# Decoding the MLP weights in half-width pieces inside the rounds, and moving reload transfers to GpSimd's queue

## The chip, the cores and the metric

One core of one Trainium2 chip runs one program. The metric is the device time of one execution in microseconds (us). The engines are TensorE (PE, matmul; PEld is its weight load), VectorE (DVE), ScalarE (ACT), GpSimd (POOL) and SyncE (SP, which here only starts transfers). Each engine works through its own list of instructions in order. A transfer (DMA) is started from the list of one engine, and an engine that waits to start one holds up everything behind it on its list.

## The reference

Attention with a sigmoid, a gated layer, then a residual MLP. The change touches the last part alone:

```python
x = moe(attention(q, k, v))              # (4, 448, 768)
xn = (x - mean) / sqrt(var + 1e-6) * g_ln
out = x + maximum(xn @ w_ch1, 0) @ w_ch2   # w_ch1 768x3072, w_ch2 3072x768
```

The weights arrive as float64. The kernel sees them as pairs of 32-bit words and makes float32 of them on the chip ("decode").

## The kernel before

The matmuls are done in three passes (`mm3`, lines 268 to 271): each float32 operand is split in a high and a low part (`split`: a copy on ACT, line 298, and a subtraction, line 299 on DVE or line 733 on GpSimd).

**The rounds.** `mlp` runs 24 rounds: two halves `h` of the tokens, and in each half twelve groups `g` of hidden columns (`GF * g` and the next). A round `k` makes the group's hidden activations by seven products `P_` (a Strassen-Winograd form: L11, L12, S2, S1, S3, L22, S4, each 9 matmuls of 448 columns) and, between and after them, the seven chunks of the second matrix multiply for the round before (`ch2_chunks`: 12 matmuls of 384 columns per chunk, then one addition of the 128x768 result onto `y`, line 790 on DVE). In a common round the first chunk (c1) stands between the products S3 and L22 and the other six (c2 to c7) follow the last product. Two buffers (`ps2`) hold chunk results, so the matmuls of c4 can start only when the addition of c2 is done, those of c5 after c3's addition, and so on. A round is followed in the trace from one copy of line 863 to the next.

**The decoded weights.** Each weight is a 128x768 block. The first half of the tokens needs every group's four blocks (two of `w_ch1`, two of `w_ch2`) decoded; decoded blocks are written to a scratch tensor `wscr` and read back by `Weight.load` (line 723), for both halves. Groups 0 to 4 are decoded during the attention phase. Groups 5 to 11 (28 blocks) are decoded in rounds 1 to 10 by the jobs of `pre_jobs`: `load` (line 279, 768 KB from `in_w`), `decode` (`w_decode`: line 287 on ACT, then lines 288, 289 and 292 on DVE) and `store` (line 348, 384 KB). `pre.pop(n)` takes the next n jobs and writes their instructions into the lists of the engines at that place. Before the change there is one raw buffer (`pre_start`), so a step is decode, store, load of the next block, and the rounds hold nine pops, that is three blocks a round. The order of the instructions is written out by hand (`manual_schedule`).

**What is queued on SP.** The store waits for the decode and the load waits for the raw buffer; behind them on SP's list stand the `Weight.load`s of the round: `w2c.load`, `w2d.load` and the next round's two (`nxt.load`).

**The handover between the halves.** In round 11 (`h` = 0, the last group) `ops_load` (line 1125) replaces each operand of the products by that of the other half, 1344 KB each, seven in all, as soon as its product is done. Round 12 starts with six chunks of round 11, whose sums go to the output (line 796), then `y_load` (line 1155) reads the other half's `y`, seven times 384 KB. All of these are started by SP.

Of the kernel before, what the change touches and what calls it, by code (L numbers as in the profile page):

```python
# [11 lines left out]
F32 = mybir.dt.float32  # L12
# [22 lines left out]
GF = 2  # L35
# [126 lines left out]
class Ring:  # L162
# [4 lines left out]
    def next(self):  # L167
        self.i += 1
        return self.blocks[(self.i - 1) % len(self.blocks)]
# [54 lines left out]
def sigmoid_attention_gmlp_mlp(ctx: ExitStack, tc, q, k, v, w_in, w_sp, w_out, g_ln, w1, w2, out):  # L224
# [50 lines left out]
    dec_r = Ring(F, WC, 2)  # L275

    def w_load(src, ring=raw_r):
        raw = ring.next().bits(WC, 2)
        nc.sync.dma_start(raw.rearrange("p n t -> p (n t)"), src.bitcast(U32))
        return raw  # L280

    def w_decode(raw, blk=None):
        blk = blk or dec_r.next()
        f, bits = blk.ap(WC), blk.bits(WC)
        low, high = raw[:, :, 0], raw[:, :, 1]

        nc.scalar.mul(f, high.bitcast(F32), 2.0**-112)  # L287
        nc.vector.tensor_scalar(bits, bits, 3, None, op0=ALU.logical_shift_left)  # L288
        nc.vector.scalar_tensor_tensor(  # L289
            bits, low, 29, bits, op0=ALU.logical_shift_right, op1=ALU.bitwise_or  # L290
        )
        nc.vector.scalar_tensor_tensor(  # L292
            bits, high, 0x80000000, bits, op0=ALU.bitwise_and, op1=ALU.bitwise_or
        )
        return f
# [38 lines left out]
    def pre_jobs(todo, raws, decs):  # L334

        raw, f = {}, {}
        n = len(todo)

        def load(w, i):
            raw[w, i] = w_load((w1, w2)[w][i], raws)  # L340

        def decode(w, i):
            blk = decs.next()
            f[w, i] = blk.ap(WC)
            w_decode(raw.pop((w, i)), blk)

        def store(w, i):
            nc.sync.dma_start(wscr[w, i], f.pop((w, i)))

        if len(raws.blocks) > 1:  # L350
            steps = (load, 0), (store, 3), (decode, 2)
        else:
            steps = (decode, 1), (store, 1), (load, 0)
        for m in range(n + 3):
            for job, i in steps:
                if 0 <= m - i < n:
                    yield functools.partial(job, *todo[m - i])
                else:
                    yield idle

    def weights_of(groups):
        return [(w, GF * g + i) for g in groups for w in range(2) for i in range(GF)]

    jobs = Jobs()

# [400 lines left out]
    def mlp(first, proj, after):  # L766
# [58 lines left out]
        for k, (h, g) in enumerate(todo):  # L825
# [48 lines left out]
            if k == 0:  # L874
                left.put("S4")
                proj.turn()
                nxt.sums(nc.vector)
            P_(pa, "S2", "T2", False)
            nc.scalar.copy(tb, pa[:, :S])
            pre.pop(1)  # L880
            pd = ps1()
            P_(pd, "S1", "T1", True)
            pre.pop(2)
            if nxt and k:
                nxt.sums()
            P_(pa, "S3", "T3", False)
            nc.scalar.copy(tc_, pa[:, :S])
            nc.vector.tensor_add(tc_, pd[:, :S], tc_)
# [5 lines left out]
            if k:  # L894
                w2c.load()
                if nxt:
                    nxt.put("L11")
            P_(pa, "L22", "T4", False)
            put(1, 0, pa[:, :S])
            if nxt:  # L900
                nxt.put("L12" if k else "S2")
# [1 line left out]
            P_(pd, "S4", "R22", False)  # L903
            nc.vector.tensor_add(tb, pd[:, :S], tb)  # L904
            put(0, 1, tb)
            pre.pop(2)
            if k == 0:
                nxt.put("S1", "S3")
                w2c.load()
                w2d.load()  # L910
                y_start()
                nxt.put("L22", "S4")
                w2c.split()
                w2d.split()
                pre_start()
            else:
                if h and g == 0:
                    for c in range(HCH):
                        y_load(1, c)
                if nxt:  # L920
                    nxt.put("S2")
                next(chunks, None)
                if nxt:
                    nxt.put("S1", "S3")
                next(chunks, None)
                if nxt:
                    nxt.put("L22", "S4")
                w2d.load()
                next(chunks, None)
                pre.pop(1)  # L930
                next(chunks, None)
                w2c.split()
                next(chunks, None)
                pre.pop(2)
                for _ in chunks:
                    pass
                late = w2d
            chunks, pend = ch2_chunks(h, g, hb, second), True
            left = nxt
# [30 lines left out]
    pv_load(1)  # L970
    jobs.pop(1)
    pre = Jobs()
    pre.add(pre_jobs(weights_of(range(NPRE)), p_raw, p_dec))
    for i in range(2 * n_pairs):
        p, t = divmod(i, 2)
        now[0] = i
# [144 lines left out]
    def ops_load(name):  # L1121

        n = OPS.index(name)
        place, at = PLACE_OPS[n]
        nc.sync.dma_start(R.tiles[place][:, at : at + OPW].bitcast(F32), oscr[n])

    ops_at(*range(6))
    proj = Project(wo, gb, ys_r, xn_r, stage_r, t_b, t4_b)
# [22 lines left out]
    ys = [None] * HCH  # L1151
    pre = Jobs()

    def y_load(h, c):
        nc.sync.dma_start(ys[c].ap(DM), yscr[h * HCH + c])

    def y_start():

# [6 lines left out]

    def pre_start():
        raws, decs = Ring(F, 0, 0), Ring(F, 0, 0)
        raws.blocks, decs.blocks = [F.at("mlp", 3072, 2 * WC)], [F.at("mlp", 4608, WC)]
        decs.blocks.append(next(t for t in dec.q if t.key == "mlp"))
        dec.q.remove(decs.blocks[1])  # L1170
        pre.add(pre_jobs(weights_of(range(NPRE, NGRP)), raws, decs))

    mlp(left, proj, after)

# [46 lines left out]
```

## Time and profile before

| | us |
|---|---|
| median of 3 runs | 1169.75 (1168.42 to 1169.81) |
| the profiled execution | 1166.97 |
| its span (first to last instruction) | 1165.2 |
| TensorE busy | 1082.0 (93%) |
| VectorE busy | 674.5 (58%) |
| ScalarE busy | 457.1 (39%) |
| GpSimd busy | 315.7 (27%) |

Busy times are unions over the span. A busy TensorE is not necessarily at full speed: the granted clock (1.00 is 2.4 GHz, 0.50 is 1.2 GHz) has to be read beside it. Positions are given in us from the start of the span. The table of stages gives for each stretch the busy time of each engine and the clock; the rows of the order of time show which instruction ended an engine's idle time, in brackets.

### The profile page before, as it was taken

To read this page: it belongs to the slowest core of one execution; us is meant where nothing else is said; L and a number is where in the kernel's file an instruction comes from. 1 tells how busy PE (TensorE), PEld (TensorE's weight loads), DVE (VectorE), ACT (ScalarE), POOL (GpSimd) and SP (SyncE) were. 2 spreads that over 40 slices of the span, in tenths; PEclk is the share of its full clock that TensorE was granted. 3 is DMA by queue.
4 is the path that set the end of the run, shared out by engine and by line. 5 is a ranking of instruction groups with operands and counts; after the bars stand their busy time and mean duration, and the time that the engine had idled before them with its cause. 6 is when DMAs were issued, how large, how long until landed. Compare 5 with 4: busy or idle time off the path is not lost.

```text
span 1165.2 us, 14921 instructions
## 1 busy us (share of the span) xinstructions
PE 1082.0 (93%) x5644; PEld 950.1 (82%) x5644; DVE 674.5 (58%) x988; ACT 457.1 (39%) x792; POOL 315.7 (27%) x278
## 2 busy tenths in 40 slices
PE   8999999999999689888898788898899999999997
PEld 4566666679899578788898788898799999999997
DVE  4734536446767757676666676654355555555543
ACT  6755556554566643233222233230322332333310
POOL 1322212212047433122233022322133222222210
PEclk9999999999999889989988889998999999999999
DMA  8756779735224673534443534366521111111103
GB/s 236 232 176 215 246 235 332 233 141 188 75 83 175 240 270 122 176 120 165 141 158 122 176 119 166 133 245 232 196 68 55 55 55 55 55 58 65 55 28 95
DMA packets 65112, 174.52 MB, mean 150 GB/s; under 512 B 11664, under 2 KB 23312, under 8 KB 64016
## 3 DMA queue, kind: packets, MB, share of 16 engines
q1 hardware_dynamic: 62320, 164.11, 41.9%
q0 software_dynamic: 1600, 7.34, 1.9%
q10 hardware_dynamic: 1120, 2.11, 0.5%
q8 instruction: 44, 0.72, 0.3%
q14 instruction: 28, 0.23, 0.1%
HBM read 126.67 MB, written 46.87 MB: 149 GB/s over the span
## 4 chain that ended last, share of the span: by engine, by line
PE 63%; DVE 11%; DMA 10%; issue 5%; ACT 5%; POOL 3%; SPq 2%; POOLq 0%; ACTq 0%; DVEq 0%
PE ps L269 18%; PE ps L270 17%; PE ps L271 17%; PE ps L463 5%; PE ps L447 5%; DMA f_mlp<-in_w 4%; DMA f_base<-wscr 2%; DVE f_mlp L289 2%; DVE f_mlp L292 2%; DVE f_mlp L288 2%; ACT f_mlp L287 1%; ACT f_mlp L678 1%; DMA sscr<-vraws 1%; DVE f_base L790 1%; DMA wscr<-f_att 1%
## 5 line engine op out<-in xcount | busy, mean ns | idle before, releaser
L269 PE MATMUL ps<-r_mlp,r_base 128*128 128x384 f32 (+1 forms) x946 | 340.6, 360 | 55.3 <-DVE f_base L790 41.2
L270 PE MATMUL ps<-r_mlp,r_base 128*128 128x384 f32 (+1 forms) x946 | 336.7, 356 | 2.6 <-POOL r_mlp L733 2.6
L271 PE MATMUL ps<-r_mlp,r_base 128*128 128x384 f32 (+1 forms) x946 | 336.2, 355 | 0.0
L269 PEld LDWEIGHTS ps<-r_mlp,r_base 128*128 128x128 f32 x946 | 186.9, 198 | 66.1 <-DVE f_base L790 44.4
L733 POOL TENSOR_TENSOR r_mlp<-f_base,r_mlp 128x768 fp32r<-128x768 f32 x48 | 88.4, 1843 | 529.2 <-ACT r_mlp L732 529.2
L270 PEld LDWEIGHTS ps<-r_mlp,r_base 128*128 128x128 f32 x946 | 186.8, 197 | 6.9 <-POOL r_mlp L733 3.3
L271 PEld LDWEIGHTS ps<-r_mlp,r_base 128*128 128x128 f32 x946 | 186.4, 197 | 3.0
L790 DVE TENSOR_TENSOR f_mlp<-ps,f_mlp 128x768 f32<-128x768 f32 (+1 forms) x97 | 91.6, 947 | 78.0 <-PE ps L271 77.7
L269 PE MATMUL ps<-r_base 128*128 128x448 f32 (+1 forms) x348 | 132.4, 380 | 1.3 <-ACT r_base L298 1.3
L271 PE MATMUL ps<-r_base 128*128 128x448 f32 (+1 forms) x348 | 130.1, 374 | 0.4 <-DVE r_base L299 0.4
L270 PE MATMUL ps<-r_base 128*128 128x448 f32 (+1 forms) x348 | 129.9, 373 | 0.0
L451 ACT ACTIVATE f_att<-ps,bias_s 128x896 f32<-128x896 f32 x96 | 91.5, 1006 | 25.9 <-PE ps L447 25.5
L863 ACT COPY f_base<-ps 128x448 f32<-128x448 f32 x24 | 12.8, 533 | 221.5 <-PE ps L271 221.5
L790 DVE TENSOR_TENSOR f_base<-ps,f_base 128x768 f32<-128x768 f32 x72 | 68.6, 953 | 30.7 <-PE ps L271 29.9
L850 ACT ACTIVATE r_base<-f_base 128x448 fp32r<-128x448 f32 x72 | 41.6, 578 | 113.2 <-DVE f_base L904 54.4
L447 PEld LDWEIGHTS ps<-r_att 64*128 64x128 f32 x576 | 49.8, 184 | 36.9 <-issue 19.7
L447 PE MATMUL ps<-r_att 64*128 64x448 f32 x576 | 73.7, 383 | 6.4 <-ACT f_att L451 4.4
L269 PEld LDWEIGHTS ps<-r_base 128*128 128x128 f32 x348 | 65.5, 188 | 15.5 <-issue 6.5
L463 PE MATMUL ps<-f_att 128*64 128x448 f32 x384 | 77.5, 545 | 0.0
L434 POOL TENSOR_TENSOR r_att<-f_att,r_att 128x512 fp32r<-128x512 f32 x22 | 29.9, 1359 | 174.9 <-DVE r_att L430 147.0
L271 PEld LDWEIGHTS ps<-r_base 128*128 128x128 f32 x348 | 65.6, 189 | 8.6 <-DVE r_base L299 0.8
L851 DVE SCALAR_TENSOR_TENSOR r_base<-f_base,r_base 128x448 fp32r<-128x448 f32 x72 | 50.5, 701 | 37.2 <-ACT r_base L850 37.2
(127 smaller groups left out, 1551.1 us busy)
## 6 DMA issues: line engine op xcount, KB each, us to landing
f_base<-wscr SPq DMA_DIRECT2D x95, 384.0 KB, 5.0
f_mlp<-in_w SPq DMA_DIRECT2D x28, 768.0 KB, 4.8
f_att<-in_w SPq DMA_DIRECT2D x20, 768.0 KB, 5.6
wscr<-f_mlp SPq DMA_DIRECT2D x28, 384.0 KB, 2.6
wscr<-f_att SPq DMA_DIRECT2D x20, 384.0 KB, 6.0
f_att<-in_v SPq DMA_DIRECT2D x24, 256.0 KB, 5.4
f_base<-in_w_in SPq DMA_DIRECT2D x8, 768.0 KB, 4.7
f_att<-in_k SPq DMA_DIRECT2D x45, 128.0 KB, 5.2
```

The source lines that it names most:

```text
L269: nc.tensor.matmul(ps, lh, rh, start=first, stop=False, **more)
L270: nc.tensor.matmul(ps, lh, rl, start=False, stop=False, **more)
L271: nc.tensor.matmul(ps, ll, rh, start=False, stop=last, **more)
L288: nc.vector.tensor_scalar(bits, bits, 3, None, op0=ALU.logical_shift_left)
L434: eng.tensor_sub(kl, kr, kh)
L447: nc.tensor.matmul(ps[:, j, :S], a[w][rows, kc], a[x][rows], start=(i == 0), stop=(i == 2))
L451: nc.scalar.activation(af, ps[:, :, :S], AF.Sigmoid, bias=bias_s, scale=1.0 / math.sqrt(D))
L463: nc.tensor.matmul(a["ps"][rows, :S], a["v"][:, 4 * j + c], af[:, j], start=(c == 0), stop=(c == 3))
L733: nc.gpsimd.tensor_sub(self.lo, self.blk.ap(WC), self.hi)
L790: nc.vector.tensor_add(y[:, hs], ps, y[:, hs])
L850: nc.scalar.activation(hi, src, AF.Relu)
L851: nc.vector.scalar_tensor_tensor(lo, src, 0.0, hi, op0=ALU.max, op1=ALU.subtract)
```

## The change

Jobs work on a piece, a slice of 384 columns of a block, instead of the whole block. `pre_start` cuts the same memory into two raw buffers and four decoded ones. The steps become decode of piece m-2, store of piece m-2, load of piece m. The rounds hold 18 pops instead of nine (six pieces, which are three blocks), set so that a decode is popped alone and a store and a load together. `ops_load` and the second half's `y_load` are started by GpSimd instead of SP. The decoding in the attention phase keeps whole blocks and its order (`weights_of(..., WC)`, three raw buffers).

```diff
 def w_load(src, ring=raw_r):
-        raw = ring.next().bits(WC, 2)
+        raw = ring.next().bits(src.shape[-1], 2)
 def w_decode(raw, blk=None):
         blk = blk or dec_r.next()
-        f, bits = blk.ap(WC), blk.bits(WC)
+        n = raw.shape[1]
+        f, bits = blk.ap(n), blk.bits(n)
 def pre_jobs(todo, raws, decs):
-        def load(w, i):
-            raw[w, i] = w_load((w1, w2)[w][i], raws)
+        def load(w, i, cols):
+            raw[w, i, cols] = w_load((w1, w2)[w][i][:, cols], raws)
...
-        if len(raws.blocks) > 1:
+        if len(raws.blocks) > 2:
             steps = (load, 0), (store, 3), (decode, 2)
         else:
-            steps = (decode, 1), (store, 1), (load, 0)
+            steps = (decode, 2), (store, 2), (load, 0)
...
-    def weights_of(groups):
-        return [(w, GF * g + i) for g in groups for w in range(2) for i in range(GF)]
+    def weights_of(groups, n):
+        cuts = [slice(o, o + n) for o in range(0, WC, n)]
+        return [(w, GF * g + i, cut) for g in groups for w in range(2) for i in range(GF) for cut in cuts]
 def mlp(first, proj, after):                # one round
+            pre.pop(1)
             P_(pa, "S2", "T2", False)
             nc.scalar.copy(tb, pa[:, :S])
-            pre.pop(1)
             P_(pd, "S1", "T1", True)
             pre.pop(2)
...
+            pre.pop(1)
             P_(pa, "S3", "T3", False)
...
             P_(pa, "L22", "T4", False)
+            pre.pop(2)
             put(1, 0, pa[:, :S])
...
             pre.pop(1)
             P_(pd, "S4", "R22", False)
             nc.vector.tensor_add(tb, pd[:, :S], tb)
             put(0, 1, tb)
-            pre.pop(2)
...
                     for c in range(HCH):
-                        y_load(1, c)
+                        y_load(1, c, nc.gpsimd)
+                pre.pop(2)
                 nxt.put("S2")
                 next(chunks, None)          # c2
+                pre.pop(1)
                 nxt.put("S1", "S3")
                 next(chunks, None)          # c3
+                pre.pop(2)
                 nxt.put("L22", "S4")
                 w2d.load()
                 next(chunks, None)          # c4
                 pre.pop(1)
                 next(chunks, None)          # c5
                 w2c.split()
+                pre.pop(2)
                 next(chunks, None)          # c6
-                pre.pop(2)
+                pre.pop(1)
                 for _ in chunks: pass       # c7
+                pre.pop(2)
 def ops_load(name):
-        nc.sync.dma_start(R.tiles[place][:, at : at + OPW].bitcast(F32), oscr[n])
+        nc.gpsimd.dma_start(R.tiles[place][:, at : at + OPW].bitcast(F32), oscr[n])
 def pre_start():
-        raws.blocks, decs.blocks = [F.at("mlp", 3072, 2 * WC)], [F.at("mlp", 4608, WC)]
-        decs.blocks.append(next(t for t in dec.q if t.key == "mlp"))
-        dec.q.remove(decs.blocks[1])
-        pre.add(pre_jobs(weights_of(range(NPRE, NGRP)), raws, decs))
+        raws.blocks = F.at("mlp", 3072, 2 * WC).cut(WC, WC)
+        decs.blocks = F.at("mlp", 4608, WC).cut(HALF, HALF)
+        last = next(t for t in dec.q if t.key == "mlp")
+        dec.q.remove(last)
+        decs.blocks += last.cut(HALF, HALF)
+        pre.add(pre_jobs(weights_of(range(NPRE, NGRP), HALF), raws, decs))
```

## Rows read from the trace of the kernel before

**Rows 1.** Stages: us, busy of PE, PEld, DVE, ACT, POOL, granted clock, DMA share, GB/s.

```profile
424.60:771.00 346.40, 301.71 (x1463) 286.28 (x1464) 232.06 (x294) 105.61 (x188) 90.85 (x61) 0.91 0.42 150
771.00:868.20 97.20, 88.05 (x443) 83.53 (x442) 44.47 (x63) 24.65 (x49) 23.54 (x18) 0.95 0.57 205
868.20:1117.50 249.30, 249.30 (x1325) 239.93 (x1324) 134.86 (x189) 73.92 (x145) 72.33 (x54) 1.00 0.17 58
```

**Rows 2.** Order of time in round 6: start, length, instruction, idle before and its releaser.

```profile
606.59 0.37 SPq L279 DMA_DIRECT2D f_mlp<-in_w  x1
611.10 0.91 ACT L287 ACTIVATE f_mlp<-f_mlp 128x768 f32<-128x768 f32 x1 [2.24 <-DMA f_mlp<-in_w]
612.03 0.56 DVE L288 TENSOR_SCALAR f_mlp<-f_mlp 128x768 uint32<-128x768 uint32 x1 [2.45 <-ACT f_mlp L287]
614.50 0.62 DVE L904 TENSOR_TENSOR f_base<-ps,f_base 128x448 f32<-128x448 f32 x1
616.77 0.95 DVE L790 TENSOR_TENSOR f_base<-ps,f_base 128x768 f32<-128x768 f32 x1
617.77 0.69 PE L269 MATMUL ps<-r_mlp,r_base 128*128 128x384 f32 x1 [3.82 <-DVE f_base L790]
```

**Rows 3.** Waits over the span: who for whom, us in total, times, longest.

```profile
ACT f_mlp L287 <- DMA f_mlp<-in_w: 43.9, 18, 4.8
```

**Rows 4.** TensorE's gaps in rounds 2 and 1, and the stretches behind them.

```profile
488.52 0.44 PE L269 MATMUL ps<-r_mlp,r_base 128*128 128x384 f32 x1 [1.17 <-DVE f_mlp L790]
488.50:492.80 4.30, 4.28 (x23) 4.13 (x24) 1.79 (x2) 0.00 (x0) 0.00 (x0) 1.00 1.00 333
444.41 0.45 PE L269 MATMUL ps<-r_mlp,r_base 128*128 128x384 f32 x1 [2.00 <-DVE f_base L790]
445.40:448.80 3.40, 3.40 (x12) 3.40 (x12) 2.60 (x5) 1.64 (x2) 0.55 (x1) 0.50 0.37 148
```

**Rows 5.** Groups by shape, whole span: count, busy us, mean ns, idle before.

```profile
L790 DVE TENSOR_TENSOR f_mlp<-ps,f_mlp 128x384 f32<-128x384 f32 x2 | 1.1, 558 | 0.6 <-PE ps L271 0.5
```

**Rows 6.** VectorE in round 15, which decodes nothing, in order of time.

```profile
908.20 0.55 DVE L299 TENSOR_TENSOR r_base<-f_base,r_base 128x384 fp32r<-128x384 f32 x1
908.88 0.62 DVE L904 TENSOR_TENSOR f_base<-ps,f_base 128x448 f32<-128x448 f32 x1
...
911.16 0.95 DVE L790 TENSOR_TENSOR f_base<-ps,f_base 128x768 f32<-128x768 f32 x1
912.03 1.02 DVE L299 TENSOR_TENSOR r_base<-f_base,r_base 128x384 fp32r<-128x384 f32 x2
913.11 0.96 DVE L790 TENSOR_TENSOR f_base<-ps,f_base 128x768 f32<-128x768 f32 x1
913.99 1.26 DVE L299 TENSOR_TENSOR r_base<-f_base,r_base 128x384 fp32r<-128x384 f32 x1
...
917.35 0.96 DVE L790 TENSOR_TENSOR f_mlp<-ps,f_mlp 128x768 f32<-128x768 f32 x1 [0.77 <-PE ps L271]
919.47 0.96 DVE L790 TENSOR_TENSOR f_mlp<-ps,f_mlp 128x768 f32<-128x768 f32 x1 [1.16 <-PE ps L271]
```

**Rows 7.** Order of time, rounds 12 and 13: TensorE's gaps, SP's first `y` loads.

```profile
800.34 0.69 PE L269 MATMUL ps<-r_mlp,r_base 128*128 128x384 f32 x1 [3.04 <-ACT r_mlp L732]
802.23 0.69 PE L270 MATMUL ps<-r_mlp,r_base 128*128 128x384 f32 x1 [1.20 <-POOL r_mlp L733]
830.83 1.41 SPq L1155 DMA_DIRECT2D f_base<-yscr  x3
844.13 0.47 PE L269 MATMUL ps<-r_mlp,r_base 128*128 128x448 f32 x1 [3.99 <-ACT f_base L879]
```

**Rows 8.** Chain of waits: start, length, the transfers of rounds 11 and 13.

```profile
784.51 14.85 DMA f_base<-wscr
...
834.78 7.54 DMA f_base<-wscr
```

**Rows 9.** Line 279 in rounds 2 to 10: us from issue to landing.

```profile
DMA to landing us min/median/max: 4.4/4.8/7.0
```

**Rows 10.** Line 1030, GpSimd's own transfers of 768 KB: issue ns, min/median/max.

```profile
L1030 POOL DMA_DIRECT2D f_mlp<-vscr x4: 762/786/925, 249.6 to 284.8; - x4
```

More of the change, by code (lines that the diff above doesn't have):

```diff
@@ L337, in pre_jobs, with decode, store @@
         n = len(todo)
-        def load(w, i):
-            raw[w, i] = w_load((w1, w2)[w][i], raws)
-        def decode(w, i):
+        def load(w, i, cols):
+            raw[w, i, cols] = w_load((w1, w2)[w][i][:, cols], raws)
+        def decode(w, i, cols):
             blk = decs.next()
[L344 to L348, printed above, removed]
-        if len(raws.blocks) > 1:
+            w_decode(raw.pop((w, i, cols)), blk)
+            f[w, i, cols] = blk.ap(cols.stop - cols.start)
+        def store(w, i, cols):
+            nc.sync.dma_start(wscr[w, i][:, cols], f.pop((w, i, cols)))
+        if len(raws.blocks) > 2:
             steps = (load, 0), (store, 3), (decode, 2)
         else:
-            steps = (decode, 1), (store, 1), (load, 0)
+            steps = (decode, 2), (store, 2), (load, 0)
         for m in range(n + 3):
@@ L972, in sigmoid_attention_gmlp_mlp @@
     pre = Jobs()
-    pre.add(pre_jobs(weights_of(range(NPRE)), p_raw, p_dec))
+    pre.add(pre_jobs(weights_of(range(NPRE), WC), p_raw, p_dec))
     for i in range(2 * n_pairs):
@@ L1152, in sigmoid_attention_gmlp_mlp, with y_load @@
     pre = Jobs()
-    def y_load(h, c):
-        nc.sync.dma_start(ys[c].ap(DM), yscr[h * HCH + c])
+    def y_load(h, c, eng=nc.sync):
+        eng.dma_start(ys[c].ap(DM), yscr[h * HCH + c])
     def y_start():
```

## The prediction

> **What bounds the kernel now.** I read the stages first [rows 1]. Rounds 14 to 22 decode nothing: 249.30 us for nine rounds, 27.7 each, with TensorE busy for every one of them at full clock. That is the floor for a round. Rounds 1 to 10, which decode, take 346.40 us, 34.6 each, and 69.4 above ten such rounds. Two things make it up: 44.7 us in which TensorE has nothing to do (346.40 less 301.71 busy), and 24.7 us because it is busy longer (301.71 against 277) at a granted clock of 0.91. Rounds 11 to 13 take 97.20 against 83.1: 9.2 us idle and 5.0 of slow clock. So 83.5 us lie above the floor, all of it between 424.6 and 868.2, and nothing the change does reaches another stretch: the attention phase keeps its whole blocks.
>
> Next, the order of time in one round shows the idle part's cause [rows 2]. A block's load is issued at 606.59 once the decode before it is done; ScalarE waits for it 2.24 us, until 611.10; VectorE waits behind that 2.45 us, until 612.03; the addition for S4 (line 904), which depends on none of this, stands behind the decode on VectorE's list and starts at 614.50; c2's addition starts at 616.77; TensorE, whose c4 needs that chunk buffer, has been idle for 3.82 us by 617.77. Such a gap stands in each of rounds 1 to 10, ten in all, the first at 444.41 [rows 4]. The waits say the same in total: line 287 waited 43.9 us for its data, 18 times [rows 3]. The slow clock follows from the gap: after one of 2.00 us the next stretch is granted 0.50 for 3.4 us, after one of 1.17 it stays at 1.00 [rows 4].
>
> **The change, rounds 1 to 10.** *Removed:* the wait of line 287. With two raw buffers the piece that is decoded was asked for two steps earlier. A round has six steps, about 5 us apart, so a load has about 5 us or more between the end of the decode that frees its buffer and its own decode (two steps, less the decode's time and SP's issue). A whole block lands in 4.4 to 7.0 us, 4.8 in the middle [rows 9]; half as many bytes shouldn't take longer. I take the wait as zero; if the middle value held for pieces too, most turns would still fit, and at 7.0 the tightest would wait some 2 us once a round.
>
> *Added:* fixed cost. One block's three VectorE operations run from 612.03 to 614.50, 2.47 us [rows 2]. An addition of 384 columns takes 0.558 us [rows 5], one of 768 takes 0.95 [rows 2]: 0.39 for the columns and 0.17 fixed. Line 288 halves from 0.56 to 0.17 + 0.20 = 0.37. So a piece costs 0.37 + 0.56 + 0.56, about 1.45 us with the overlap of neighbours. Bounds: half of 2.47, 1.24, and, where GpSimd works at the same time, more: in round 15 the split at 913.99 took 1.26 us beside one of GpSimd's, against 0.55 for the like one at 908.20 [rows 6], so I allow up to 0.7 more a piece. ScalarE's half needs no cover: it is busy 106 of 346 us [rows 1].
>
> *VectorE's room.* In 346.40 us it is busy 232.06, 23.2 a round; six pieces in place of three blocks add 6 x 1.45 less 3 x 2.47, 1.3, giving 24.5 of 27.7. On the average it fits, but not in each place. In round 15 line 904 starts at 908.88, c2's addition at 911.16, c3's at 913.11 [rows 6]; from c5 on, VectorE waits for TensorE (0.77, then 1.16), and these additions come 2.12 us apart, the length of a chunk. Now a piece (1.45) stands ahead of line 904 and one more (1.45) between the additions of c2 and c3. The first uses the 0.2 us that are free there (the split at 908.20, then 908.88) and moves line 904, and with it c2's addition, by 1.24: it ends at 913.4, c4 could start when c3's matmuls ended, at 913.1, and waits 0.3. The second moves c3's addition to 915.7 (911.16 + 1.24 + 0.87 to the next start + 1.45 + 1.02 for two splits), it ends at 916.6, c5 could start at 915.5 (913.4 + 2.12) and waits 1.1. The pieces after c4 and c6 find VectorE 0.8 to 1.2 us early per chunk and cost at most 0.7 when GpSimd's split of `w2c` lands on them; the first two pieces of a round fall before line 888, where ScalarE's copies leave VectorE idle. So the gaps add 1.4 to 2.1 us: a round of 29.1 to 29.8, I take 29.5. The gaps are 0.3 and 1.1, near the 1.17 that left the clock alone [rows 4], so I give no slow clock. Ten rounds: 295, plus 1.5 for the gap at the start of round 1, which waits on `w_ch2` and stays: 296.5, a gain of 49.9.
>
> **The change, rounds 11 to 13.** In round 11 a `Weight.load` started at 784.51 lands after 14.85 us [rows 8], since operands of 1344 KB each are on SP's queue ahead of it. TensorE waits 3.04 and 1.20 for its split [rows 7]. In round 12 SP starts seven `y` loads from 830.83 on [rows 7], the next `Weight.load` only at 834.78, and that takes 7.54 us [rows 8]; TensorE then waits 3.99 [rows 7]. On GpSimd's list the `y` loads can start as their blocks are written out, mostly before 830, and the operands no longer stand ahead of the small loads on SP's. GpSimd pays 0.79 us per start, as in its own transfers of 768 KB [rows 10], 14 x 0.79 = 11 us in all. It is busy 23.54 of 97.20 us [rows 1]. Its starts wait for TensorE to be through with each operand; behind them are the splits of `w2c` and `w2d` and the sums for the next products. Four starts stand ahead of the sums, so these come some 3.2 us later, and they are wanted only for the next round's operands. Cost: zero to 3.2, I take 1, nearer to zero, as GpSimd is idle three quarters of this time. Of the 14.1 us above the floor 8.2 are the three gaps, 5.0 the slow clock that follows; the rest stays. Gain: 13.2 less 1, 12.
>
> A rule speaks against this part. All transfers go over the same 16 engines however they are started, and starting on several lists saves only issue time, says the Trainium skill (DMA: Bandwidth & Descriptors, Issuing engines are not separate DMA queues). By it the sum would be 1116. Whether the 14.85 us are a queue's order or the engines' share, no row of before can tell; it is rival 3.
>
> **Sum.** 49.9 + 12 = 61.9 us. The profiled execution took 1166.97, the median of the runs is 1169.75; from the median: 1107.9. I predict 1108.
>
> **Rivals.**
> 1. *No room is lost:* the adds of c2 and c3 come in time and a round is 27.7. For it: VectorE's average room of 3 us. Against: the two places above. 277 + 1.5 in place of 296.5: 18 more, 1090.
> 2. *The clock falls all the same.* Two gaps that lie 2 us apart and add up to 1.4 to 2.1 may count as the single one of 2.00 did. A halved stretch of 3.4 us costs 1.7, two cost 3.4: over nine rounds 15 to 31, 1123 to 1139, most likely 1125.
> 3. *The handover keeps its contention.* The small loads share the engines with the same bytes as before, now even at the same time. Then only SP's time for the `y` loads comes back (834.78 less 830.83, 3.95), 12 becomes 4: 1116.
> 4. *Slower: loads that come late set the pace.* With two raw buffers and six pieces each buffer turns three times a round. A turn is the landing time T, 0.6 for line 287, 1.45 for the decode, 0.7 for SP's store and load. Rounds of 35.8 (34.6 plus the handover's 1.2 per round) would give back everything: T = 35.8 / 3 - 2.75 = 9.2 us. From there it is slower; at the 14.85 of [rows 8] a round is 52.8, and the time 1340. Against: 4.4 to 7.0 for blocks of twice the size [rows 9]. It decides only if shorter rows land much worse, or if the small loads between them hold the pieces up.
>
> **How the numbers follow.** Forecast 0.48 (1100 to 1117), rival 1 0.10, rival 2 0.22, rival 3 0.14, rival 4 0.06. The likeliest gives 1108. The range takes in the forecast, rivals 1 to 3 and the bound of a round that waits 2 us for its tightest load (1128): 1090 to 1138, leaving out rival 4 and the tails of 1 and 2. Two parts in a thousand (2.3 us) is about what a measurement of this kernel can tell from no change; all cases but rival 4 are far beyond it: faster 0.93, same 0.02, slower 0.05.
>
> **What would show it.** Right: line 287's wait for `in_w` falls from 43.9 us to a few; lines 288, 289, 292 appear 56 times, near 0.4, 0.6 and 0.6 us apart from contention; rounds 2 to 10 are 29 to 30 us at a clock of 0.98 or more, with gaps below 1.5 us released by line 790; no TensorE gap above 1 us in rounds 11 to 13. Wrong: gaps that end on a transfer of `in_w` (step one), gaps of 2 us released by line 790 with the clock at 0.50 behind them (rival 2), line 732 still waiting for `wscr` at the handover (rival 3), or splits of GpSimd late behind its starts.

## The result and the profile after

The changed kernel takes 1115.89 us (median of 4 runs, 1114.5 to 1116.91) against 1169.78 before: a ratio of 0.954, interval 0.9523 to 0.9556. The forecast was 1108, with a range of 1090 to 1138; the gain is 53.9 us where 61.9 were expected. The profiled execution took 1114.5 us, with a span of 1112.7, 52.5 shorter than before's. One execution of an experiment below, `split_copy_first`, took 2008.04 us, far outside its other three, and is left out of the times and ratios given for it.

The stages of after, with the columns of [rows 1]: rounds 1 to 10, rounds 2 to 9 of them, rounds 11 to 13.

```profile
426.50:730.20 303.70, 286.22 (x1463) 264.26 (x1464) 250.12 (x378) 108.13 (x217) 88.83 (x61) 0.99 0.52 171
457.80:699.20 241.40, 229.34 (x1178) 211.45 (x1177) 204.37 (x312) 88.61 (x177) 70.62 (x48) 1.00 0.53 170
730.20:816.20 86.00, 83.63 (x443) 79.84 (x442) 43.93 (x63) 24.59 (x48) 30.85 (x32) 1.00 0.65 232
```

| stretch | before | after | saved | forecast |
|---|---|---|---|---|
| up to round 1 | 424.6 | 426.5 | -1.9 | 0 |
| rounds 1 to 10 | 346.4 | 303.7 | 42.7 | 49.9 |
| rounds 11 to 13 | 97.2 | 86.0 | 11.2 | 12 |
| rounds 14 to 22 | 249.3 | 249.3 | 0 | 0 |
| round 23 and the end | 47.7 | 47.2 | 0.5 | 0 |
| span | 1165.2 | 1112.7 | 52.5 | 61.9 |

The first row lies in the attention phase, whose code is the same in both; 1.9 us there is a difference between two executions. Of the rest of the shortfall 7.2 us lie in rounds 1 to 10 and 0.8 in rounds 11 to 13; the end came out 0.5 ahead. The clock, 0.91 there before, is 0.99, and the third stage has its full clock too.

*The wait.* Line 287 of before is line 288 now, and the lines 288, 289, 292 of VectorE are 289, 290, 293. The waits of after (who for whom, us in total, times, longest):

```profile
ACT f_mlp L288 <- DMA f_mlp<-in_w: 32.5, 10, 4.0
...
PE ps L269 <- DVE f_base L793: 14.8, 20, 2.5
...
ACT r_mlp L735 <- DMA f_base<-wscr: 0.3, 1, 0.3
```

The first looks as if little had changed (43.9 in [rows 3]). The groups by shape of after (count, busy us, mean ns, idle of the engine just before) show who still pays for it:

```profile
L293 DVE SCALAR_TENSOR_TENSOR f_mlp<-f_mlp 128x384 uint32<-128x384 uint32 x56 | 42.6, 760 | 1.9
L290 DVE SCALAR_TENSOR_TENSOR f_mlp<-f_mlp 128x384 uint32<-128x384 uint32 x56 | 39.2, 701 | 1.9
L289 DVE TENSOR_SCALAR f_mlp<-f_mlp 128x384 uint32<-128x384 uint32 x56 | 26.9, 481 | 0.0
```

VectorE's first decode instruction, which stands behind line 288, is never kept waiting (0.0): the wait is ScalarE's alone, which runs one piece ahead and has time. Round 3 in order of time, with the columns of [rows 2]:

```profile
500.78 0.35 DVE L289 TENSOR_SCALAR f_mlp<-f_mlp 128x384 uint32<-128x384 uint32 x1
...
502.23 0.62 DVE L909 TENSOR_TENSOR f_base<-ps,f_base 128x448 f32<-128x448 f32 x1
...
505.51 0.45 PE L269 MATMUL ps<-r_mlp,r_base 128*128 128x384 f32 x1 [0.26 <-DVE f_base L793]
...
507.36 0.37 SPq L279 DMA_DIRECT2D f_mlp<-in_w  x1
507.38 2.16 POOL L736 TENSOR_TENSOR r_mlp<-f_base,r_mlp 128x768 fp32r<-128x768 f32 x1 [10.33 <-ACT r_mlp L735]
507.57 0.34 PE L271 MATMUL ps<-r_mlp,r_base 128*128 128x384 f32 x1
...
508.77 0.44 PE L269 MATMUL ps<-r_mlp,r_base 128*128 128x384 f32 x1 [0.87 <-DVE f_base L793]
509.05 0.34 PE L270 MATMUL ps<-r_mlp,r_base 128*128 128x384 f32 x1
...
511.33 0.56 ACT L288 ACTIVATE f_mlp<-f_mlp 128x384 f32<-128x384 f32 x1 [4.03 <-DMA f_mlp<-in_w]
511.34 0.44 PE L269 MATMUL ps<-r_mlp,r_base 128*128 128x384 f32 x1 [0.18 <-DVE f_mlp L793]
...
514.64 0.35 DVE L289 TENSOR_SCALAR f_mlp<-f_mlp 128x384 uint32<-128x384 uint32 x1
```

The load issued at 507.36 lands at 511.3; ScalarE has waited 4.03 us for it, but VectorE wants the piece only at 514.64, 2.8 us after line 288 is done. What is left of TensorE's 3.82 us gap [rows 2] are short ones that end on the additions of c2 to c5 (line 793).

*The handover.* TensorE's only gap over 1 us in rounds 11 to 13, and the first of the seven `y` loads, now GpSimd's (the last starts at 786.68):

```profile
758.26 0.44 PE L270 MATMUL ps<-r_mlp,r_base 128*128 128x384 f32 x1 [1.45 <-POOL r_mlp L736]
...
765.06 0.57 POOL L1164 DMA_DIRECT2D f_base<-yscr  x1
```

Of the gaps in [rows 7] the 3.04 is gone, the 1.20 is 1.45 and the 3.99 is gone. The `Weight.load`s of this stretch land in 2.9 us at least, 3.6 in the middle and 10.9 at most, in before in 2.8, 7.1 and 14.8 (this line of after, then that of before):

```profile
DMA to landing us min/median/max: 2.9/3.6/10.9
```

```profile
DMA to landing us min/median/max: 2.8/7.1/14.8
```

### The profile page after: what moved, and what is told of

Same layout as the page of the kernel before. It is cut to its first block, busy times and chain, and to the rows that moved or that the text cites. A ratio compares the mean times of both kernels' runs of the same rounds, so it can differ in the third digit from the quotient of the medians.

```text
span 1112.7 us, 15188 instructions
## 1 busy us (share of the span) xinstructions
PE 1064.4 (96%) x5644; PEld 926.0 (83%) x5644; DVE 690.8 (62%) x1072; ACT 459.4 (41%) x820; POOL 321.3 (29%) x292
## 4 chain that ended last, share of the span: by engine, by line
PE 67%; DVE 16%; issue 7%; ACT 4%; POOL 3%; DMA 2%; SPq 0%; POOLq 0%; DVEq 0%; ACTq 0%
PE ps L269 19%; PE ps L270 18%; PE ps L271 18%; PE ps L466 6%; PE ps L450 5%; DVE f_mlp L290 3%; DVE r_base L300 2%; DVE r_base L854 2%; DVE f_mlp L289 2%; DVE r_mlp L300 2%; DVE f_base L793 2%; DVE f_mlp L293 2%; ACT r_base L853 1%; ACT f_mlp L681 1%; DVE f_mlp L793 1%
## 5 line engine op out<-in xcount | busy, mean ns | idle before, releaser
L269 PE MATMUL ps<-r_mlp,r_base 128*128 128x384 f32 (+1 forms) x946 | 331.6, 351 | 21.0 <-DVE f_base L793 14.8
L270 PE MATMUL ps<-r_mlp,r_base 128*128 128x384 f32 (+1 forms) x946 | 326.4, 345 | 2.9 <-POOL r_mlp L736 2.9
L271 PE MATMUL ps<-r_mlp,r_base 128*128 128x384 f32 (+1 forms) x946 | 325.9, 345 | 0.0
L736 POOL TENSOR_TENSOR r_mlp<-f_base,r_mlp 128x768 fp32r<-128x768 f32 x48 | 91.8, 1914 | 424.4 <-ACT r_mlp L735 424.4
L269 PEld LDWEIGHTS ps<-r_mlp,r_base 128*128 128x128 f32 x946 | 178.4, 189 | 37.8 <-DVE f_base L793 21.2
L270 PEld LDWEIGHTS ps<-r_mlp,r_base 128*128 128x128 f32 x946 | 178.5, 189 | 7.0 <-POOL r_mlp L736 3.4
L271 PEld LDWEIGHTS ps<-r_mlp,r_base 128*128 128x128 f32 x946 | 178.4, 189 | 2.9
L269 PEld LDWEIGHTS ps<-r_base 128*128 128x128 f32 x348 | 65.5, 188 | 15.6 <-issue 6.5
L271 PEld LDWEIGHTS ps<-r_base 128*128 128x128 f32 x348 | 65.6, 189 | 8.7 <-DVE r_base L300 0.8
L270 PEld LDWEIGHTS ps<-r_base 128*128 128x128 f32 x348 | 65.7, 189 | 6.6
```

The costliest lines, as they stand in the source:

```text
L269: nc.tensor.matmul(ps, lh, rh, start=first, stop=False, **more)
L270: nc.tensor.matmul(ps, lh, rl, start=False, stop=False, **more)
L271: nc.tensor.matmul(ps, ll, rh, start=False, stop=last, **more)
L736: nc.gpsimd.tensor_sub(self.lo, self.blk.ap(WC), self.hi)
```

## The experiments

Each was timed beside the kernel before (1172 to 1174 us in these sets), and ratios are against it. `y_on_sp` was run once.

### Each part alone

`queues_only` is before with `ops_load` and the second half's `y_load` started by GpSimd; `decode_only` is after with both given back to SP.

```diff
-                        y_load(1, c, nc.gpsimd)
+                        y_load(1, c)
-        nc.gpsimd.dma_start(R.tiles[place][:, at : at + OPW].bitcast(F32), oscr[n])
+        nc.sync.dma_start(R.tiles[place][:, at : at + OPW].bitcast(F32), oscr[n])
```

> The kernel before with one part of the change: the operands of the other half and its y are started by GpSimd, the decoding stays as it was. My theory: in the changed kernel rounds 11 to 13 took 86.0 us against 97.2, and these 11.2 us come from the queues alone, so 1169.8 - 11 = about 1158.5 us, ratio near 0.990, and no TensorE gap above 1.5 us in rounds 11 to 13, with rounds 1 to 10 still at 346 us. Rival (transfers share the engines, only SP's time for the y loads comes back): 3 to 4 us, about 1166, and line 732 still waits for wscr in round 12.

> The changed kernel with the operands and y started by SP again. My theory: the two parts add up, so rounds 1 to 10 stay near 303.6 us, rounds 11 to 13 go back to 97 us, and the time is about 1115.9 + 11 = 1127 us. Rival (the handover became better because the decoding ends earlier or leaves SP's queue freer): rounds 11 to 13 stay below 92 us and the time is 1116 to 1121.

`queues_only`: 1160.27 us, ratio 0.9902 (0.9878 to 0.9926). `decode_only`: 1125.89, 0.9609 (0.9588 to 0.963). Stages of the first, rounds 1 to 10 and 11 to 13, then the same of the second:

```profile
425.60:777.10 351.50, 301.59 (x1463) 285.50 (x1464) 233.06 (x294) 105.41 (x189) 91.42 (x61) 0.92 0.43 148
777.10:863.20 86.10, 83.73 (x443) 79.85 (x442) 44.21 (x63) 24.58 (x49) 30.76 (x32) 1.00 0.65 232
```

```profile
426.30:730.00 303.70, 287.44 (x1463) 265.30 (x1464) 246.46 (x378) 108.41 (x216) 87.62 (x61) 0.99 0.53 171
730.00:827.60 97.60, 88.28 (x443) 83.70 (x442) 44.45 (x63) 24.65 (x49) 23.57 (x18) 0.95 0.57 204
```

Each part works in its own stage: 86.1 and 303.7 stand as in after (86.0 and 303.7), 97.6 as in before (97.2). Rounds 1 to 10 of `queues_only` are 351.5 us long in this execution, 5 more than in before: the blocks of line 279 landed in 5.2 us in the middle in rounds 2 to 10 (4.8 in [rows 9]), and line 287 waited 47.6 us for them (43.9 in [rows 3]). Why they landed later is open. By medians the parts save 11.9 and 46.3 us, 58.2 together, where after saved 53.9 beside other runs of before (1169.78, here 1172.14); taken against 1169.78 the parts make 53.4, so they add up within the scatter of the runs. In `decode_only` line 735 waits again for its small loads in rounds 11 to 13, where after has 0.3 in all:

```profile
ACT r_mlp L735 <- DMA f_base<-wscr: 17.4, 3, 7.1
```

### The operands or `y`

`y_on_sp` gives SP the `y` loads alone (the first two lines of the diff above).

> The changed kernel with the second half's y started by SP again, the operands still by GpSimd. My theory: the two moves act at two places. The operands decide round 11 (42.3 us with them on GpSimd, 46.7 without), the y loads decide round 13 (26.8 with, 33.9 without). So round 11 stays at 42.3, round 13 goes back to 31 to 34 us with a TensorE gap of about 4 us, and the time is 1121 to 1123 against 1115.9. Rival (one of them did it all): round 13 stays at 26.8 and the time at 1116, or round 11 is worse too.

1120.95 us. Its rounds 11 and 13, then, in order of time, SP's loads of `y`, the `Weight.load`s behind them and TensorE's gap:

```profile
730.40:772.80 42.40, 40.96 (x221) 39.37 (x220) 20.52 (x27) 9.07 (x18) 17.17 (x18) 1.00 0.83 311
789.80:822.60 32.80, 27.99 (x140) 26.56 (x141) 16.27 (x22) 8.04 (x17) 9.78 (x7) 0.95 0.40 145
```

```profile
784.98 1.43 SPq L1164 DMA_DIRECT2D f_base<-yscr  x3
...
789.29 25.92 SPq L726 DMA_DIRECT2D f_base<-wscr  x7
...
798.58 0.48 PE L269 MATMUL ps<-r_mlp,r_base 128*128 128x448 f32 x1 [4.28 <-ACT f_base L883]
```

The operands decide round 11, which has its full clock, and `y` decides round 13, where the gap of 4.28 with a clock of 0.95 is back. Both transfers had to leave SP's list.

### Two pieces ahead, or only smaller ones

`one_raw` keeps the pieces and their places but has one raw buffer, so that a load is issued after the decode before it, as in the kernel before.

```diff
-            steps = (decode, 2), (store, 2), (load, 0)
+            steps = (decode, 1), (store, 1), (load, 0)
-        raws.blocks = F.at("mlp", 3072, 2 * WC).cut(WC, WC)
+        raws.blocks = F.at("mlp", 3072, 2 * WC).cut(WC)
```

> The changed kernel with one raw buffer of half width: each piece is asked for when the piece before it is decoded, one step ahead in place of two; pieces and places stay. My theory (the second buffer's lead is what removed the wait): the pieces that stand close together wait 3 to 4 us each for their data, line 287's wait for in_w comes back at some 60 us or more in total, a round is 33 to 36 us and the time 1150 to 1180. Rival (smaller pieces and more places would have done it alone): a round stays below 31.5 us and the time below 1130.

1185.04 us, ratio 1.0115 (1.0096 to 1.0134): 1.2% slower than before, and above the 1150 to 1180 expected. Rounds 1 to 10, and the wait:

```profile
425.60:801.60 376.00, 306.72 (x1463) 279.38 (x1464) 234.01 (x378) 109.16 (x216) 78.19 (x61) 0.94 0.43 138
```

```profile
ACT f_mlp L288 <- DMA f_mlp<-in_w: 191.6, 56, 6.2
```

Every one of the 56 pieces is waited for. This is the mechanism of the slower rival with one buffer in place of two: a turn is 3.3 us of landing (the median here, as in after) and the 2.75 that the prediction put beside it, 6.05; six turns make 36.3 us, and a round took 37.6. So the gain comes from the lead; in these places, pieces without it cost more than they bring.

The counterpart, whole blocks with more time between their decodes, was tried as `whole_spread`: one full-width raw buffer, decodes ahead of S2, after c4 and after c7 and nowhere else.

```diff
-            steps = (decode, 2), (store, 2), (load, 0)
+            steps = (decode, 1), (store, 1), (load, 0)
-        raws.blocks = F.at("mlp", 3072, 2 * WC).cut(WC, WC)
-        decs.blocks = F.at("mlp", 4608, WC).cut(HALF, HALF)
+        raws.blocks, decs.blocks = [F.at("mlp", 3072, 2 * WC)], [F.at("mlp", 4608, WC)]
...
             pre.pop(1)
             P_(pa, "S2", "T2", False)
...
-            pre.pop(1)
             P_(pa, "S3", "T3", False)
...
                 next(chunks, None)          # c4
                 pre.pop(1)
+                pre.pop(2)
...
                 for _ in chunks: pass       # c7
+                pre.pop(1)
                 pre.pop(2)
```

> The changed kernel with whole blocks and one raw buffer of full width in the same memory, three decodes a round, each with its store and next load at once, spread over the round: ahead of S2, after c4's addition and after c7's. The queues as in the change. My theory (what counts is that a load has its landing time before its decode, pieces are the means to get two loads into the memory): the turn of one buffer, about 4.8 us to land, 0.9, 2.47 and 0.7, is 8.9 us and three fit in 27.7 only just, so waits for in_w remain at 10 to 40 us in total, a round is 30 to 32.5 us and the time 1116 to 1140. Rival (without pieces the wait is as long as before wherever the decodes stand): rounds near 34.6 us, time near 1158.

1182.25 us, ratio 1.0092 (1.0073 to 1.0111): a miss, 0.9% slower than before. In order of time:

```profile
544.90 0.89 ACT L288 ACTIVATE f_mlp<-f_mlp 128x768 f32<-128x768 f32 x1 [4.97 <-DMA f_mlp<-in_w]
545.69 0.52 ACT L883 COPY f_base<-ps 128x448 f32<-128x448 f32 x1
...
546.26 0.74 PE L269 MATMUL ps<-r_mlp,r_base 128*128 128x448 f32 x1 [6.98 <-ACT f_base L883]
```

The copy after S2 (line 883), which TensorE needs, stands on ScalarE behind a line 288 that waits for its block; TensorE is idle for 6.98 us, ten times for 60 us in all. I had given no thought to ScalarE's list, since it is busy for a third of the time. The places after c7 and ahead of S2 lie too close together for one buffer. Whether whole blocks in better places would do as well as pieces stays open; what is shown is that the waits of line 288, which hold up no instruction of TensorE in after (32.5 us in all), do so here, where a copy for TensorE is next on the list: in the rows above a wait of 4.97 us makes a gap of 6.98.

### The gaps that are left: moving the pieces

By the prediction the rounds keep some 2 us because two pieces stand ahead of the additions for S4 and c3. `late_pieces` moves the last four pieces of a round behind the additions of c4, c5, c6 and c7, each followed by its store and load.

```diff
-            pre.pop(1)
             P_(pd, "S4", "R22", False)
...
-                pre.pop(2)
                 nxt.put("S2")
                 next(chunks, None)          # c2
-                pre.pop(1)
                 nxt.put("S1", "S3")
                 next(chunks, None)          # c3
-                pre.pop(2)
...
                 next(chunks, None)          # c4
                 pre.pop(1)
+                pre.pop(2)
                 next(chunks, None)          # c5
+                pre.pop(1)
                 w2c.split()
                 pre.pop(2)
                 next(chunks, None)          # c6
                 pre.pop(1)
+                pre.pop(2)
                 for _ in chunks: pass       # c7
+                pre.pop(1)
                 pre.pop(2)
```

> The changed kernel with the four decodes of a round's second part moved: none ahead of the addition for S4 and none between the additions of c2 and c3; one each after the additions of c4, c5, c6 and c7, each with its store and load at once. My theory: the 2.4 us that a round still lies above 27.7 (30.1) come from the two pieces that stand ahead of the additions of c2 and c3, so the gaps released by those go and a round is 27.8 to 28.8, the time 1095 to 1106. Two pieces are now close behind each other with two raw buffers, so line 287 may wait for in_w again, by some us per round, off the chunks' path. Rival (VectorE has no room for six pieces wherever they stand, or the late loads hold ScalarE's copy of the next L11): rounds stay at 30 us or more and the time at 1114 or more.

1105.74 us (1105.51 to 1106.41), ratio 0.9439 (0.9422 to 0.9456): the fastest kernel here that does all the work, 10 us below after, and within the time expected. Its rounds 2 to 9, then one of them in order of time:

```profile
454.20:692.40 238.20, 228.77 (x1178) 211.17 (x1176) 204.92 (x313) 88.18 (x177) 71.93 (x48) 1.00 0.54 173
```

```profile
532.00 2.66 DVE L300 TENSOR_TENSOR r_mlp<-f_base,r_mlp 128x384 fp32r<-128x384 f32 x2
532.05 2.19 POOL L736 TENSOR_TENSOR r_mlp<-f_base,r_mlp 128x768 fp32r<-128x768 f32 x1 [5.33 <-ACT r_mlp L735]
...
535.58 0.44 PE L269 MATMUL ps<-r_mlp,r_base 128*128 128x384 f32 x1 [0.74 <-DVE f_mlp L793]
```

The gap at c5 is gone from all eight rounds and that at c4 from four of them (it is 0.2 to 0.3 us in three and 0.96 in one), which confirms their cause. A round is 29.8 us, though, not 27.8 to 28.8: a new gap of 0.6 to 0.75 us stands at c6, where two splits of VectorE take 2.66 us beside GpSimd's split of `w2c` (1.02 for two in [rows 6]), and in six rounds one of 0.2 to 0.3 behind the copy of L11.

Not all of the 10 us lies where pieces were moved. The profiled execution's span is 9.0 us shorter than after's, and of these 3.2 lie in rounds 2 to 9, 2.2 in round 10 (28.8 us in place of 31.0), 1.8 in round 1 (29.5 in place of 31.3) and 1.8 ahead of round 1, where no piece stands yet. In the last two the clock differs: from 400 us to round 1 it is 0.86 here and 0.75 in after, and behind the gap at the start of round 1 (2.26 us here, 2.25 in after) it stayed at 1.00, where after has 0.50. Whether that comes from the places is open.

### Chasing the last gap: four moves that failed

`late_split` is `late_pieces` with `w2c.split()` behind c6's piece, out of the way of those splits. `late2` moves it too, and puts the pieces later still: after c3, c5 and c6, and the next round's first behind the copy of L11, with stores and loads one step earlier. `split_copy_first` and `late2_copy_first` are these two with S2 and its copy ahead of L12's addition and `put`.

```diff
# late_split, on late_pieces
-                w2c.split()
...
                 pre.pop(1)
+                w2c.split()
                 pre.pop(2)
                 for _ in chunks: pass       # c7
# late2, on after: at the start of a round
             nc.scalar.copy(ta, pa[:, :S])
+            pre.pop(1)
...
# the two with the copy first
             P_(pb, "L12", "R21", True)
+            if k:
+                P_(pa, "S2", "T2", False)
+                nc.scalar.copy(tb, pa[:, :S])
             nc.vector.tensor_add(ta, pb[:, :S], ta)
...
```

> late_pieces with one more edit: w2c.split stands after c6's decode in place of before c6's matmuls. In late_pieces a round was 29.7 us: the gap of 0.7 to 0.9 us at c6 was released by c4's addition, which stood behind a split of VectorE that took 2.19 us while GpSimd subtracted for w2c. My theory (the two engines get in each other's way when both read two operands from SBUF): the gap at c6 goes, a round is 28.6 to 29.2 us and the time 1097 to 1102. Rival (VectorE is simply full there): the gap stays and the time is 1105 or more.

> The changed kernel with its late decodes after the additions of c3, c5 and c6 and the sixth behind the copy of the next round's first product, w2c.split after the third of them, and the jobs begun one step earlier. My theory: no piece stands ahead of an addition that TensorE waits for, and decodes are spread so that two raw buffers suffice, so a round is 27.9 to 28.6 us, time 1091 to 1098. Rival (six pieces don't fit in VectorE's list without a wait): rounds stay at 29 us or more and the time at 1103 or more.

> late_split with the product S2 and the copy of its result on ScalarE written ahead of the addition and the hidden part of L12. In late_split the gap had moved: c4 to c6 waited less, but TensorE waited 1.7 to 2.0 us a round for the copy after S2 (line 883), which stood on ScalarE's list behind line 853, that waits for VectorE's late addition for L12. My theory (the late decodes are harmless if nothing that TensorE needs stands behind them): this gap goes, a round falls from 30.7 to 28.4 to 29.2 us and the time from 1117 to 1096 to 1104. Rival (VectorE's list is full and the lateness only comes out at the next place): a gap of 1 to 2 us shows elsewhere, rounds stay at 30 us or more and the time at 1110 or more.

> late2 with the same edit (S2 and its copy ahead of the addition and the hidden part of L12). late2's rounds were 29.9 us, with 0.8 to 1.4 us of it in the wait for that copy and 0.5 at a chunk. My theory: the copy's gap goes, a round is 28.3 to 29.1 us and the time 1098 to 1106, from 1114. Rival (the lateness comes out elsewhere): 1110 or more.

All four missed: `late_split` took 1116.98 us (ratio 0.953, 0.9511 to 0.9549), `late2` 1114.26 (0.9514, 0.9495 to 0.9532), `split_copy_first` 1111.25 to 1114.65 (0.9499, 0.9463 to 0.9534) and `late2_copy_first` 1114.47 (0.9511, 0.9491 to 0.9532). Each time the gap went on to another place. In the waits of `late_split` and then of `late2` it ends on the copy after S2 (line 883, in `late2` 884); with that copy put first it ends on the copy after S3 (9.1 us in nine waits) and on the chunks' additions (9.0 in nine) in `split_copy_first`, and on the addition behind the copy after S3 (11.0 in ten) in `late2_copy_first`:

```profile
PE ps L269 <- ACT f_base L883: 19.8, 10, 2.2
```

```profile
PE ps L269 <- ACT f_base L884: 11.6, 11, 2.5
```

What stays the same is VectorE's list. The groups of rounds 2 to 9 on VectorE, first of `late_pieces`, then of `late2` (in after the two splits of line 300 have means of 670 and 656, lines 293 and 290 have 765 and 710; line 875, which waits for TensorE, has 22.1 us idle before it there):

```profile
L300 DVE TENSOR_TENSOR r_base<-f_base,r_base 128x384 fp32r<-128x384 f32 x35 | 31.5, 920 | 0.0
...
L290 DVE SCALAR_TENSOR_TENSOR f_mlp<-f_mlp 128x384 uint32<-128x384 uint32 x48 | 26.8, 559 | 1.7
...
L854 DVE SCALAR_TENSOR_TENSOR r_base<-f_base,r_base 128x448 fp32r<-128x448 f32 x24 | 22.7, 945 | 10.3 <-ACT r_base L853 10.3
...
L289 DVE TENSOR_SCALAR f_mlp<-f_mlp 128x384 uint32<-128x384 uint32 x48 | 17.0, 354 | 18.5 <-ACT f_mlp L288 18.0
L875 DVE TENSOR_TENSOR f_base<-ps,f_base 128x448 f32<-128x448 f32 x8 | 4.9, 618 | 0.0
```

```profile
L293 DVE SCALAR_TENSOR_TENSOR f_mlp<-f_mlp 128x384 uint32<-128x384 uint32 x48 | 46.8, 976 | 1.7
L290 DVE SCALAR_TENSOR_TENSOR f_mlp<-f_mlp 128x384 uint32<-128x384 uint32 x48 | 46.2, 962 | 1.7
...
L289 DVE TENSOR_SCALAR f_mlp<-f_mlp 128x384 uint32<-128x384 uint32 x48 | 22.3, 465 | 6.0 <-ACT f_mlp L288 6.0
L300 DVE TENSOR_TENSOR r_base<-f_base,r_base 128x384 fp32r<-128x384 f32 x35 | 18.5, 550 | 0.0
```

`late_pieces` took away the 22.1 us in which VectorE waited for TensorE (line 875: now 0.0). What is left over eight rounds is 204.92 us busy, 18.5 behind line 288, 10.3 for the hand-off of `put` and 4.6 in small pieces, 1.1 of them for TensorE: the 238.2 us themselves. VectorE hardly waits for TensorE any more; its own list and its data are the round. `late2` brought the 18.5 down to 6.0, but its pieces stand beside GpSimd's work and lines 290 and 293 take 0.96 and 0.98 us where they took 0.56; VectorE is busy 219.13 us in place of 204.92, and the 12.5 gained are more than given back.

### Is it GpSimd's reading beside VectorE

`late2_no_sums` and `after_no_sums` leave out GpSimd's four sums per round in the first half, so that their products are made of old values.

```diff
-                nxt.sums()
+                nxt.sums(None if h == 0 else nc.gpsimd)
```

> late2 with GpSimd's four sums per round (lines 753 to 756) left out in the first half's rounds from 1 on; the operands S1 to S4 are then made of old values. In late2 VectorE waits for TensorE only 0.16 us a round, is busy 27.3 of 30.0 us, and 5.8 of these lie above the shortest time of each instruction. My theory (VectorE's list is what a round lasts there, and part of its length is the instructions that last longer beside GpSimd's): without the sums 2 to 4 us of VectorE's time go, a round falls to 27.8 to 28.8 us, the time from 1114 to 1094 to 1104. Rival (the collisions fill idle time and the order of waits sets the round): rounds stay at 29.5 us or more, time at 1108 or more.

> The changed kernel with the same sums left out in the first half's rounds from 1 on. There the sums fall beside the first two pieces of a round, where VectorE has 2.9 us to spare. My theory: their collisions are hidden, the gaps at c4 and c5 stay, a round goes from 30.2 to 29.6 to 30.1 us and the time from 1116 to 1110 to 1115. Rival (collisions with the sums set the round here too): a round below 29.2 us, the time below 1107.

`late2_no_sums`: 1103.75 us, ratio 0.9412 (0.9388 to 0.9436); `after_no_sums`: 1116.28, 0.9515 (0.9489 to 0.9542). Rounds 2 to 9 of the first:

```profile
458.80:690.70 231.90, 225.40 (x1178) 212.17 (x1177) 201.75 (x313) 86.89 (x176) 31.15 (x16) 1.00 0.55 177
```

Without the sums `late2`'s VectorE is busy 17.4 us less over eight rounds (219.13 to 201.75), though VectorE's own instructions are the same, and a round is 1.0 us shorter, 8.2 over the eight; most of the rest went into the wait for line 288 (13.9 us in place of 6.0). The kernel as changed was expected at 1110 to 1115 and gains nothing by the same cut. Six of its rounds 2 to 9 take 30.0 us in the mean, within the 29.6 to 30.1 expected (30.2 in after), which fits the 22.1 us that its VectorE still waits for TensorE: there a collision takes up waiting time. So the collision and its price in a full list are shown; why it is free in the other list is argued from that wait. The sums are not all of the excess: a round of 29.0 stays 1.3 above the floor.

In the other two of these rounds a longer gap made things worse, the one that after has in round 10: two splits of VectorE fall beside GpSimd's split of `w2c` and take 2.67 us (567.09), ahead of c3's addition. The gap in order of time, and the round it belongs to:

```profile
570.68 0.69 PE L269 MATMUL ps<-r_mlp,r_base 128*128 128x384 f32 x1 [2.53 <-DVE f_base L794]
```

```profile
548.30:580.50 32.20, 29.34 (x149) 27.75 (x148) 23.77 (x39) 11.03 (x22) 3.66 (x2) 0.95 0.49 158
```

The round is 32.2 us where the one before it is 30.0, with a clock of 0.95: 1.55 us more idle and 0.69 more busy. This is not the second rival, which had two short gaps bring the clock down: those left it at 1.00 in rounds 2 to 9 of after, and here a single gap is 2.53 us long.

## Why the prediction was right, point by point

- *The bound.* Right: rounds 14 to 22 are the floor in both kernels, and all of the gain lies in the two stretches named.
- *The wait of line 287.* Right in effect, wrong in its sign. "Falls from 43.9 us to a few" was the wrong thing to look for: 32.5 are left, but the 36.8 us that VectorE waited behind it are now 0.0. "Half as many bytes shouldn't take longer" held: in rounds 2 to 10 a piece lands in 3.3 us in the middle and 4.3 at most (4.8 and 7.0 in [rows 9]). With round 1 the worst is 8.4, and 9.3 in before. `one_raw` confirms the mechanism with its price.
- *A piece's 1.45 us.* Right: in round 3 a piece runs from 500.78 to 502.23. Contention adds 0.1 to 0.2 per instruction on the mean (481, 701 and 760 ns against 0.35, 0.56 and 0.56), within the 0.7 a piece that was allowed.
- *VectorE's room.* Right in place, too low in size; this is the term that was mis-sized. The forecast gave c4 0.3, c5 1.1 and the rest 0 to 0.7, 1.8 taken. In round 3, from start to start against the usual 0.18 between matmuls, c5 starts 508.77 - 507.57 = 1.20 after the last matmul, 1.02 too late, and the next one comes 0.28 later, 0.10 too late: 1.12. By the same reckoning c4 costs 0.53, c6 0.44 and c7 0.19. Together 2.3, over the forecast's upper end of 2.1. Rounds 2 to 9 take 30.2 us, not 29.5, and lie above the 29 to 30 that it gave as a sign of being right; this is 5.4 of the 7.2 us that are missing. Round 1 kept the gap at its start (31.3 us against 31.0 forecast). Round 10 (31.0) has 1.5 more than forecast: two splits on VectorE beside GpSimd's split of `w2c` took 2.66 us, as in `late_pieces`, and TensorE waited 2.52 for the addition behind them, though by the prediction's signs no gap was to reach 1.5. The prediction had that collision, but after c4 and c6 and at 0.7. The rows of round 10:

```profile
718.08 2.66 DVE L300 TENSOR_TENSOR r_mlp<-f_base,r_mlp 128x384 fp32r<-128x384 f32 x2
...
721.66 0.44 PE L269 MATMUL ps<-r_mlp,r_base 128*128 128x384 f32 x1 [2.52 <-DVE f_base L793]
```

- *The clock.* Right: 1.00 in rounds 2 to 9, so the second rival, given 0.22, did not come.
- *The handover.* Right, 11.2 against 12. `queues_only` shows it alone. GpSimd's starts took 0.53 to 0.61 us each, not 0.79, and the gap of 1.45 us that ends on its split stands where before had 1.20; by the prediction none above 1 us was to be left. The third rival falls: the operands still land in 10.9 us in the middle (10.2 in before), but the small loads land in 3.6 in place of 7.1, so it was their place behind the operands on SP's queue, and behind the `y` starts on its list (`y_on_sp`), that held them up, not the bytes. The Trainium skill (DMA: Bandwidth & Descriptors, Issuing engines are not separate DMA queues) says that starting on several engines saves only the time of starting. The third rival, which went by that, had 4 us come back; the measurement differs, with 11.2.
- *The first rival,* no room lost, was not met by the change, and by none of the variants either: the best mean of rounds 2 to 9 with all the work done is 29.8. The room is there on the average (25.5 of 27.7 us busy), but not where the additions stand, and waits and collisions fill it.
- *The fourth* did not occur with two buffers and is what `one_raw` shows with one.

Open: whether whole blocks could do as well, and what a round of `late2_no_sums` still has above the floor.

## What to carry to other kernels

A load that is late is cured by lead (a second buffer), and smaller pieces are only the way to pay for that buffer; alone they made this kernel slower than it was. Large reloads that nobody is in a hurry for belong on another list than the small loads that somebody waits for, even if the same engines carry both. Before moving work about on an engine that works in order, add up its list with its waits and its collisions: when that sum is the round, moving work only moves the gap.

## What the runs showed of the hardware

*A restart of TensorE costs more than the idle time listed.* In round 3 the three listed gaps make 0.26 + 0.87 + 0.18 = 1.31 us; from start to start they and the one at c7 cost 2.28. The listed idle begins at the end of the last matmul (0.34 us), though matmuls start every 0.18, and the second one behind a gap comes 0.10 late: some 0.25 us a gap.

*GpSimd slows VectorE by a factor of two and more where both read two operands from SBUF.* VectorE's split of 384 columns takes 0.55 us alone; two took 2.66 beside line 736 (1.02 for two in [rows 6]), and the mean of a group went from 559 to 962 ns when its place changed. The addition of line 793, which has one operand in PSUM, stayed at 0.95 us in every kernel. This is what the Trainium skill says (SBUF — State Buffer, Who interferes with whom): VectorE's second SBUF input comes through the interface by which GpSimd reads. The rows agree.

*The clock after a gap of 2 to 3 us goes either way.* After 2.00 us in before it was 0.50 [rows 4]; the round with 2.53 in `after_no_sums` was granted 0.95; after 2.52 in round 10 of the changed kernel, at 721.66, it stayed at 1.00:

```profile
721.70:727.10 5.40, 5.40 (x31) 5.40 (x32) 3.56 (x5) 0.00 (x0) 0.00 (x0) 1.00 0.44 149
```

`late_split` has two gaps of 2.10 us on the same copy: after the one at 493.88 the clock stayed at 1.00, after the one at 677.43 it was 0.50. The longest gap that left it at 1.00 was 2.96 us (`late_pieces`, 409.05); behind every gap above 3.0 us in the rounds of these kernels stands a stretch at 0.50. What decides for the others no run here tells.
